# Which matmuls are cut into column halves, and where beta is transposed

## The chip, the cores and the metric

The kernel runs on one core of a Trainium2 chip. The metric is the device time of one execution in microseconds, and a kernel's figure is the median of its runs. Before the change the median of three runs is 275.47 us (275.43 to 276.7).

A core has a matrix engine (TensorE, PE in the profile; its weight loads are listed as PEld), a vector engine (VectorE, DVE), a scalar engine (ScalarE, ACT), GpSimd (POOL) and a sync engine (SyncE, SP) that here only issues transfers. Transfers run on 16 DMA engines that all queues share.

## What is computed

The reference is an attention without softmax, followed by a two-layer network with a gated activation:

```python
def phi(x, c, s):
    r = np.maximum(x, 0.0)
    return np.concatenate([r * c, r * s], axis=-1)
q_p = phi(q, cos_w, sin_w)
k_p = phi(k, cos_w, sin_w)
kv = np.einsum('bhsf,bhsd->bhfd', k_p, v)
z = np.sum(k_p, axis=2)
num = np.einsum('bhsf,bhfd->bhsd', q_p, kv)
den = np.einsum('bhsf,bhf->bhs', q_p, z)[..., None] + 1e-06
...
x = np.ascontiguousarray(attn_out.transpose(0, 2, 1, 3)).reshape(B * S, H * D)
h = x @ w_in
g = h * (1.0 / (1.0 + np.exp(-beta * h)))
out = g @ w_out
```

There are 8 batches of 8 heads, 576 positions and a head size of 64; the network has 4608 tokens, 512 inputs, 2048 hidden units and 512 outputs. Everything comes in and goes out as 32-bit floats; the matrix work is done in bf16.

## The kernel before

The 4608 tokens are worked off in nine chunks of 512 (`c` = 0 to 8). While the network works on one chunk, the attention for later tokens is prepared, so that matmuls of both kinds follow each other in one hand-written order on TensorE. The kernel switches the scheduler off (`manual_schedule`): each engine runs its instructions in the order in which the Python code records them. From chunk 1 on the order is a list of short tokens (`ORDERS`), read from left to right.

The matmuls that matter here:

- `kv_mm` (line 285) and `num_mm` (line 308) are the attention. They are small: 64 rows by 64 columns of weights, 130 or 65 columns of data, 36 or more in a row. Four of them run side by side in the matrix array, so they follow each other every 5 to 20 ns.
- `h_mm` (line 400) is the first layer of chunks 0 and 1. A hidden group of 128 units takes four matmuls (`mi` = 0 to 3) into one PSUM bank of 512 columns. The parameter `cols` cuts each of them but the first into that many column pieces; with `cols` = 2 a group is one matmul of 512 columns and six of 256. Lines 921 and 942 call it with 2 for the slots 4 to 15 of both chunks.
- `o_mm` (line 559) is the second layer of chunk 0, in parts of four hidden groups (`o_part`, slots 16 to 23). `cols` works in the same way, the first hidden group excepted. Line 923 asks for 2 in slots 16 to 22 and for 1 in slot 23.
- `o_fast` (line 581) is the second layer of chunk 1, and `o_pair` (line 631) that of the chunks 2 to 8. Both use a scheme that replaces eight block products by seven. A chunk has two row pairs (`pr` = 0 and 1, the tokens `x…`/`y…` in chunk 1 and `ox…`/`oy…` later). A product is eight matmuls of 256 columns that add up in half a PSUM bank; `prod` records them, and the products of a pair come in the order 1, 2, 6, 5, 7, 3, 4 or one like it.
- `h_pair` (line 524) does the first layer of chunks 2 to 8 in the same scheme, with products of two matmuls.

Each matmul is preceded by a load of its weights, an instruction of its own. Cutting a matmul into two pieces therefore adds two instructions to TensorE's stream.

The head of the kernel works as follows. TensorE runs small matmuls on zeros (`warm_pe`) until the table of tangents is ready. It then transposes that table (line 699) and, from a 16 by 128 tile, `beta` (line 702), runs 15 more warming matmuls, and turns the first two groups of queries (`q_turn_pe`, line 244) with one more warming matmul between them. VectorE copies the transposed `beta` out of PSUM (line 706), relus the second query group, multiplies the turned queries by the tangents (line 232), inverts `beta` (line 713) and goes on with values and keys (lines 218 and 201). The tile of `beta` arrives by a transfer that ScalarE issues (line 139). Its first users are the activations of the first layer (line 408) and the scaling of the second weight matrix (line 131).

Of the kernel before, what the change touches and what calls it, by code (L numbers as in the profile page):

```python
# [16 lines left out]
P = 128  # L17
NQ = 9
EPS = 1e-6


@with_exitstack
def kernel(
# [453 lines left out]
    def fast_ops(left, right, prod, finish):  # L477
# [36 lines left out]
            "4": lambda: prod(at("b", 0), left(6), right(6), False),  # L514
        }, bank, at

    def h_pair(c, i):

        jt0 = 2 * i
        xt, n = xt_tile(c), NB // 2  # L520

        def prod(dst, l, r, start):
            for g in range(2):
                nc.tensor.matmul(dst, lhsT=l[:, g], rhs=r[:, :, g * HP : (g + 1) * HP], start=start and g == 0,  # L524
                                 stop=g == 1, skip_group_check=True)

        def w(f, jp):
            f += jt0 % 4
            return win[jt0 // 4][:, 2 * jp : 2 * jp + 2, f * P : (f + 1) * P]

        def x(jp, k_):
            return xt[:, k_ * n : (k_ + 1) * n, jp]

        s1, s2, s3, s4 = (w_sum(jt0, k_) for k_ in range(4))
        t1, t2, t3, t4 = (wx["x"][:, 4 * (c % 2) + k_] for k_ in range(4))
        lefts = (w(0, 0), s1, s2, w(0, 1), s3, s4, w(1, 1))
        rights = (x(0, 0), t1, t2, x(1, 0), t3, x(1, 1), t4)
        ops, bank, at = fast_ops(lefts.__getitem__, rights.__getitem__, prod, lambda add: add(at("b", 1)))
        ops["A"] = lambda: h_silu(c, jt0, bank("a"))
        ops["B"] = lambda: h_silu(c, jt0 + 1, bank("b"))  # L540
        return ops
# [32 lines left out]
    def o_fast(c, pr, banks):  # L574

        b_ps, a_ps, e_ps = ps[:, banks[0], 0:HM], ps[:, banks[1], 0:HM], ps[:, banks[1], HM:DM]
        tok = slice(pr * P, (pr + 1) * P)

        def prod(dst, left, right, start, stop):
            for i in range(JT // 2):  # L580
                nc.tensor.matmul(dst, lhsT=left(i), rhs=right[:, i], start=start and i == 0,  # L581
                                 stop=stop and i == JT // 2 - 1, skip_group_check=True)

        def g_part(r, hf):
            def at(i):
                jt = 2 * i + r
                return gs[c, jt // 4][:, jt % 4, hf * (TCH // 2) + pr * P : hf * (TCH // 2) + (pr + 1) * P]
            return at

        def s_part(t):  # L590
            return lambda i: t[:, i, tok]

        o1 = osb_pool.tile([P, DM], FP32, name="o_sb", tag="o_sb")
        o2 = osb_pool.tile([P, DM], FP32, name="o_sb", tag="o_sb")
        p1 = part.tile([P, HM], FP32, name="p1", tag="p1")
        p5 = part.tile([P, HM], FP32, name="p5", tag="p5")
        u = part.tile([P, HM], FP32, name="u", tag="u")

        add = dict(op=ALU.add)
        return {  # L600
            "1": lambda: prod(b_ps, g_part(0, 0), B11, True, False),
            "5": lambda: prod(e_ps, s_part(S[1]), T1, False, False),
            "6": lambda: prod(b_ps, s_part(S[2]), T2, False, False),
            "2": lambda: prod(a_ps, g_part(1, 0), B21, True, True),
            "7": lambda: prod(b_ps, s_part(S[3]), T3, False, False),
            "3": lambda: prod(e_ps, s_part(S[4]), B22, False, True),
            "4": lambda: prod(b_ps, g_part(1, 1), T4, False, True),
            "c1": lambda: nc.scalar.copy(p1, b_ps),
            "c5": lambda: nc.scalar.copy(p5, e_ps),
            "cu": lambda: nc.scalar.copy(u, b_ps),  # L610
            "c4": lambda: nc.scalar.copy(o2[:, 0:HM], b_ps),
            "a2": lambda: nc.vector.tensor_tensor(o1[:, 0:HM], a_ps, p1, **add),
            "a3": lambda: nc.vector.tensor_tensor(o1[:, HM:DM], e_ps, u, **add),
            "a7": lambda: nc.vector.tensor_tensor(o2[:, HM:DM], b_ps, p5, **add),
            "o1": lambda: store(c, pr, o1),
            "o2": lambda: store(c, pr + 2, o2),
            "p1": lambda: store(c, pr, o1, eng=nc.sync),
            "p2": lambda: store(c, pr + 2, o2, eng=nc.sync),
        }


    def o_pair(c, pr):

        last = c == NTC - 1 and pr == 1
        tok = slice(pr * P, (pr + 1) * P)
        order = (0, 1, 2, 3, 4, 5, 7, 6) if c + 1 >= B else range(JT // 2)
        sb = {}

        def prod(dst, l, r, start):
            for i in order:  # L630
                nc.tensor.matmul(dst, lhsT=l(i), rhs=r[:, i], start=start and i == 0, stop=i == order[-1],  # L631
                                 skip_group_check=True)

        def g_part(r, hf):
            def at(i):
                jt = 2 * i + r
                return gs[c, jt // 4][:, jt % 4, hf * (TCH // 2) + pr * P : hf * (TCH // 2) + (pr + 1) * P]
            return at

        def s_part(t):  # L640
            return lambda i: t[:, i, tok]

        def sb_tile(key):
            sb[key] = osb_pool.tile([P, DM], FP32, name="o_sb", tag="o_sb")
            return sb[key]

        def stored(half):
            sb["done"] = sb.get("done", 0) + 1
            if last:
                store(c, pr + 2, sb["2"], half * HM, (half + 1) * HM)  # L650
            elif sb["done"] == 2:
                store(c, pr + 2, sb["2"])

        def finish(add):
            add(sb_tile("2")[:, HM:DM])
            stored(1)

        def piece(half, eng):
            if "1" not in sb:
                sb_tile("1")  # L660
            cols = slice(half * HM, (half + 1) * HM)
            (nc.scalar.copy if eng == "act" else nc.vector.tensor_copy)(sb["1"][:, cols], at("a", half))
            store(c, pr, sb["1"], half * HM, (half + 1) * HM)

        def take(key, eng):
            copy = nc.scalar.copy if eng == "act" else nc.vector.tensor_copy
            if key == "a":
                got = copy(sb_tile("1"), bank("a"))  # L668
                store(c, pr, sb["1"])
            else:  # L670
                got = copy(sb["2"][:, 0:HM], at("b", 0))
                stored(0)
            return got

        lefts = (g_part(0, 0), s_part(S[1]), s_part(S[2]), g_part(1, 0), s_part(S[3]), s_part(S[4]), g_part(1, 1))
        rights = (B11, T1, T2, B21, T3, B22, T4)
        ops, bank, at = fast_ops(lefts.__getitem__, rights.__getitem__, prod, finish)
        ops["A"], ops["B"] = (lambda: take("a", "act")), (lambda: take("b", "act"))
        ops.update({n: lambda h=i % 2, e=("act", "dve")[i // 2]: piece(h, e) for i, n in enumerate("PQUV")})
        ops["X"], ops["Y"] = (lambda: take("a", "dve")), (lambda: take("b", "dve"))  # L680
        return ops
# [2 lines left out]
        for i in range(count):  # L684
            nc.tensor.matmul(ps[:, bank, 0:w], lhsT=zeros[:, 0:P], rhs=zeros[:, 0:w], start=True, stop=True)  # L685

    def warm_long(count):
        for i in range(count):
            nc.tensor.matmul(ps[:, 1], lhsT=zeros.bitcast(FP32)[:, 0:P],
                             rhs=raw_tile(0, "q")[:, 0, 0:8].rearrange("q n d -> q (n d)"), start=True, stop=True)  # L690

    beta = const.tile([P, JT], FP32, name="beta")
    rbeta = const.tile([P, JT], FP32, name="rbeta")

    warm_pe(54, 48)

    for bank, n0, n1 in ((6, 0, 5), (7, 5, NQ)):
        for n in range(n0, n1):
            nc.tensor.matmul(ps[:, bank, (n - n0) * HP : (n - n0 + 1) * HP],
                             lhsT=tan9[0:HP, n : n + 1].to_broadcast([HP, P]), rhs=identf,  # L700
                             is_transpose=True, start=(n == n0), stop=(n == n1 - 1))
    nc.tensor.transpose(ps[:, 1, 0:JT], beta16, identf[0:JT, 0:JT])
    for bank, n0, n1 in ((6, 0, 5), (7, 5, NQ)):
        nc.scalar.copy(tanr[:, n0:n1, :].rearrange("q n p -> q (n p)"), ps[:, bank, 0 : (n1 - n0) * HP])
    q_relu(0, 0)
    nc.vector.tensor_copy(beta, ps[:, 1, 0:JT])
    nc.vector.tensor_copy(ps[:, 0, 0:NQ], cos9)
    nc.vector.tensor_copy(ps[:, 0, 16 : 16 + NQ], sin9)
    q_relu(0, 1)
    warm_pe(6, 128, bank=2)  # L710
    warm_pe(9, 48, bank=2)
    q_turn_pe(0, 0, 4)
    nc.vector.reciprocal(rbeta, beta)
    warm_pe(1)
    take = q_turn_pe(0, 1, 2, hold=True)
    warm_long(2)
    take("act", 0)
    take("dve", 1)
    v_scale(0, 1, 0, 0, 8, eng="pool")
# [193 lines left out]
    for slot in range(32):  # L913
        if slot < 4:
            if slot == 0:
                for jt in range(2):
                    h_mm(0, jt, (2, 3), slice(0, 4))
            h_mm(0, slot, (2, 3), slice(4 if slot < 2 else 0, 8))
            h_act(0, slot)
        elif slot < 16:  # L920
            h_group(0, slot, 2 if slot < 16 else 1)
        elif slot < 24:
            o_part(0, slot % 4, (slot - 16) // 4, 2 if slot < 23 else 1)
        else:
            for tt in range(4):
                o_mm(0, tt, (slot - 16,))
# [10 lines left out]
    def h_slot(slot):  # L937
# [1 line left out]
            h_mm(1, slot, (2, 3))  # L939
            h_act(1, slot)  # L940
        else:
            h_group(1, slot, 2 if slot < 16 else 1)

    def behind_turn():
        for jp in range(2):
# [197 lines left out]
```

## Time and profile before

| what | us |
|---|---|
| median of three runs | 275.47 |
| lowest and highest run | 275.43 and 276.7 |
| the profiled execution's own time | 276.29 |
| its span, first to last instruction | 274.5 |
| TensorE busy in the span | 264.1 |
| VectorE busy | 225.9 |
| ScalarE busy | 196.3 |
| GpSimd busy | 57.0 |

The profiled execution is one run; 1.8 us of its time lie outside the span. Its costliest groups of instructions on TensorE, from the page:

```profile
L524 PE MATMUL ps<-w_stage,ws 128*128 128x256 bf16 x324 | 52.4, 273 | 0.0
L524 PE MATMUL ps<-xt,win 128*128 128x256 bf16 x216 | 37.0, 273 | 0.0
L631 PE MATMUL ps<-wout,g_t 128*128 128x256 bf16 x224 | 28.9, 273 | 0.0
L400 PE MATMUL ps<-xt,win 128*128 128x256 bf16 (+1 forms) x220 | 32.4, 306 | 0.0
```

A row names the line, the engine, what is written and read, and the shape; `x324` is the count, `52.4, 273` the busy time in us and the mean duration of one in ns, and the last number the idle time of the engine just before them. The duration of one matmul runs from its first read to its last write; matmuls overlap, so that 324 of 273 ns fill 52.4 us and not 88. What counts for the time is the distance from one start to the next.

The page also lists what the DMA queues moved. Two of them carry instructions, not data: `q8` with 30 packets of 16 KB and `q14` with 12 of 8 KB.

### The profile page before, as it was taken

How to read it: one execution, taken by the hardware profiler on the slowest of the kernel's cores; microseconds unless marked ns; L12 is line 12 of the kernel's file. 1: busy time of each engine (PE TensorE's matmuls, PEld its weight loads, DVE VectorE, ACT ScalarE, POOL GpSimd, SP SyncE). 2: the span in 40 equal slices, each digit the busy share in tenths (PEclk: the TensorE clock that was granted, in tenths of full speed). 3: DMA queues.
4: the chain of work that ended last, by engine and by line, in shares of the span. 5: the costliest groups of instructions: out<-in, count | busy, mean ns of one | idle time of the engine just before them, and what ended most of it. 6: DMA issues, size and time to landing. Idle time of an engine off the chain costs nothing.

```text
span 274.5 us, 9255 instructions
## 1 busy us (share of the span) xinstructions
PE 264.1 (96%) x3834; PEld 219.5 (80%) x3837; DVE 225.9 (82%) x596; ACT 196.3 (72%) x406; POOL 57.0 (21%) x75
## 2 busy tenths in 40 slices
PE   7799999999899999999999999989999999999994
PEld 6557775577686888888888888878888888888883
DVE  4888799999879989779989996998589868758852
ACT  5588888697648968799489967976696179428910
POOL 1420000120025000850093009300840060000000
PEclk9999999999999999999999999999999999999999
DMA  7999999999997997899499559962600660015005
GB/s 247 371 396 384 390 388 289 291 232 351 307 185 219 359 278 78 249 401 161 105 270 370 97 61 242 292 77 57 180 4 2 61 180 5 2 28 127 1 2 153
DMA packets 51754, 54.15 MB, mean 197 GB/s; under 512 B 31920, under 2 KB 32448, under 8 KB 51712
## 3 DMA queue, kind: packets, MB, share of 16 engines
q1 hardware_dynamic: 49120, 47.26, 66.0%
q0 software_dynamic: 2208, 6.03, 7.1%
q8 instruction: 30, 0.49, 0.8%
q10 hardware_dynamic: 384, 0.27, 0.4%
q14 instruction: 12, 0.10, 0.1%
HBM read 36.71 MB, written 9.44 MB: 168 GB/s over the span
## 4 chain that ended last, share of the span: by engine, by line
PE 92%; DVE 3%; DMA 2%; issue 1%; ACTq 0%; ACT 0%; DVEq 0%
PE ps L631 32%; PE ps L524 31%; PE ps L400 11%; PE ps L559 5%; PE ps L581 5%; PE ps L308 4%; PE ps L285 3%; DMA beta<-in_moe_beta_dram 2%; DVE qs L232 1%; DVE vb L218 1%; PE ps L244 1%; PE ps L368 1%; DVE rk L201 1%; PE ps L685 0%; DVE xs L331 0%
## 5 line engine op out<-in xcount | busy, mean ns | idle before, releaser
L434 ACT ACTIVATE g_t<-ps,beta 128x512 bf16<-128x512 f32 x108 | 68.1, 704 | 2.2 <-PE ps L524 1.9
L524 PE MATMUL ps<-w_stage,ws 128*128 128x256 bf16 x324 | 52.4, 273 | 0.0
L550 POOL DMA_DIRECT2D out_dram<-o_sb x46 | 24.7, 543 | 130.0 <-ACT o_sb L668 87.7
L631 PEld LDWEIGHTS <-w_stage 128*128 128x128 bf16 x448 | 43.4, 98 | 5.2
L524 PEld LDWEIGHTS <-ws 128*128 128x128 bf16 x432 | 41.8, 98 | 6.1
L500 DVE TENSOR_TENSOR ps<-ps,p 128x256 f32<-128x256 f32 x82 | 33.9, 429 | 11.8 <-ACT p L497 4.0
L524 PE MATMUL ps<-xt,win 128*128 128x256 bf16 x216 | 37.0, 273 | 0.0
L631 PEld LDWEIGHTS <-g_t 128*128 128x128 bf16 x336 | 32.3, 98 | 4.3 <-ACT g_t L434 0.4
L524 PEld LDWEIGHTS <-win 128*128 128x128 bf16 x324 | 31.5, 98 | 4.1
L400 PE MATMUL ps<-xt,win 128*128 128x256 bf16 (+1 forms) x220 | 32.4, 306 | 0.0
L493 ACT COPY ps<-ps 128x256 f32<-128x256 f32 x68 | 24.8, 386 | 8.0 <-PE ps L524 3.8
L232 POOL TENSOR_TENSOR qs<-qt,tanr 128x1152 bf16<-128x1152 bf16 (+2 forms) x10 | 16.7, 1676 | 66.3 <-ACT xt L373 33.0
L631 PE MATMUL ps<-wout,g_t 128*128 128x256 bf16 x224 | 28.9, 273 | 0.0
L400 PEld LDWEIGHTS <-win 128*128 128x128 bf16 x220 | 21.3, 98 | 9.2
L420 DVE TENSOR_TENSOR w_stage<-g_t 128x512 bf16<-128x512 bf16 x64 | 26.2, 429 | 2.1 <-ACT g_t L434 1.7
L226 ACT ACTIVATE vb<-raw_v,sin 128x256 bf16<-128x256 f32 (+1 forms) x62 | 27.6, 511 | 0.0
L408 ACT ACTIVATE g_t<-ps,beta 128x512 bf16<-128x512 f32 x36 | 23.5, 693 | 4.5 <-PE ps L400 4.4
L631 PE MATMUL ps<-wout,w_stage 128*128 128x256 bf16 x224 | 26.6, 273 | 0.0
L631 PE MATMUL ps<-T,w_stage 128*128 128x256 bf16 x224 | 26.6, 273 | 0.0
L331 DVE TENSOR_TENSOR xs<-ps,rden 128x768 bf16<-128x768 f32 (+4 forms) x26 | 24.3, 942 | 0.9 <-DVE rden L324 0.2
L228 DVE TENSOR_SCALAR vb<-raw_v,cos 128x256 bf16<-128x256 f32 x63 | 22.4, 391 | 0.0
L668 ACT COPY o_sb<-ps 128x512 f32<-128x512 f32 x12 | 6.9, 588 | 20.8 <-PE ps L631 20.8
(116 smaller groups left out, 416.5 us busy)
## 6 DMA issues: line engine op xcount, KB each, us to landing
raw_v<-in_v_dram SPq DMA_DIRECT2D x7, 1152.0 KB, 8.8
raw_k<-in_k_dram SPq DMA_DIRECT2D x7, 1152.0 KB, 11.6
raw_q<-in_q_dram SPq DMA_DIRECT2D x7, 1152.0 KB, 9.2
out_dram<-o_sb POOLq DMA_DIRECT2D x46, 128.0 KB, 4.8
w_stage<-in_moe_w_in_dram SPq DMA_DIRECT2D x6, 512.0 KB, 8.3
out_dram<-o_sb SPq DMA_DIRECT2D x22, 128.0 KB, 3.1
w_stage<-in_moe_w_out_dram SPq DMA_DIRECT2D x2, 1024.0 KB, 9.5
w_stage<-in_moe_w_out_dram SPq DMA_DIRECT2D x4, 512.0 KB, 13.8
```

Of the source, the lines that this page charges most:

```text
L226: got = nc.scalar.activation(o, a, AF.Copy, scale=t[:, n : n + 1])
L228: got = nc.vector.tensor_scalar(o, a, scalar1=t[:, n : n + 1], scalar2=None, op0=ALU.mult)
L331: nc.vector.tensor_tensor(o.rearrange("q j n s d -> q j (n s) d"), nv[:, :, a:z, :, 0:D].rearrange("q j n s d -> q j (n s) d"), rden[:, :, ...
L400: nc.tensor.matmul(ps[:, h_bank(c, jt), i * 64 : (i + w) * 64], lhsT=win[jt // 4][:, mi, (jt % 4) * P : (jt % 4 + 1) * P], rhs=xt[:, i : i ...
L408: return nc.scalar.activation(gs[c, jt // 4][:, jt % 4], ps[:, h_bank(c, jt)], AF.Silu, scale=beta[:, jt : jt + 1])
L420: return nc.vector.tensor_tensor(o, l, r, op=op)
L434: return nc.scalar.activation(gs[c, jt // 4][:, jt % 4], bank, AF.Silu, scale=beta[:, jt : jt + 1])
L493: return nc.scalar.copy(at("a", 0), at("b", 0))
L500: nc.vector.tensor_tensor(dst, at("b", 0), st["p5"], op=ALU.add)
L524: nc.tensor.matmul(dst, lhsT=l[:, g], rhs=r[:, :, g * HP : (g + 1) * HP], start=start and g == 0, stop=g == 1, skip_group_check=True)
L550: (eng or own).dma_start(out=out_v[bb, n][:, m0:m1], in_=o_sb[hf * HP : (hf + 1) * HP, m0:m1])
L631: nc.tensor.matmul(dst, lhsT=l(i), rhs=r[:, i], start=start and i == 0, stop=i == order[-1], skip_group_check=True)
```

## The change

A table at the head names the places where matmuls are cut in two; all others stay whole.

```diff
+FINE = {("h", 0): (4, 5, 12),
+        ("h", 1): (4, 6, 8, 11, 13, 14, 15),
+        ("o", 0): (20, 21, 22, 23),
+        ("p", 1, 0): (5, 6, 7),
+        ("p", 1, 1): (5, 7),
+        ("p", 3, 0): (5, 6, 7),
+        ("p", 3, 1): (4, 5, 6, 7),
+        ("p", 5, 0): (5,),
+        ("p", 5, 1): (3,)}
...
+    made = {}
+
+    def product_width(c, pr, kind="p"):
+
+        made[kind, c, pr] = made.get((kind, c, pr), 0) + 1
+        return HM // 2 if made[kind, c, pr] in FINE.get((kind, c, pr), ()) else HM
...
         def prod(dst, left, right, start, stop):
+            w = product_width(c, pr)
             for i in range(JT // 2):
-                nc.tensor.matmul(dst, lhsT=left(i), rhs=right[:, i], start=start and i == 0,
-                                 stop=stop and i == JT // 2 - 1, skip_group_check=True)
+                for m0 in range(0, HM, w):
+                    nc.tensor.matmul(dst[:, m0 : m0 + w], lhsT=left(i), rhs=right[:, i, m0 : m0 + w],
+                                     start=start and i == 0 and m0 == 0, stop=stop and i == JT // 2 - 1,
+                                     skip_group_check=True)
...
-    warm_pe(54, 48)
+    warm_pe(63, 48)
...
-    nc.tensor.transpose(ps[:, 1, 0:JT], beta16, identf[0:JT, 0:JT])
...
     q_relu(0, 0)
-    nc.vector.tensor_copy(beta, ps[:, 1, 0:JT])
...
     q_turn_pe(0, 0, 4)
+    warm_pe(1, bank=7)
+    take = q_turn_pe(0, 1, 2, hold=True)
+    nc.tensor.transpose(ps[:, 1, 0:JT], beta16, identf[0:JT, 0:JT])
+    nc.vector.tensor_copy(beta, ps[:, 1, 0:JT])
     nc.vector.reciprocal(rbeta, beta)
-    warm_pe(1)
-    take = q_turn_pe(0, 1, 2, hold=True)
-    warm_long(2)
+    warm_long(2, bank=7)
...
-            h_group(0, slot, 2 if slot < 16 else 1)
+            h_group(0, slot, 2 if slot in FINE.get(("h", 0), ()) else 1)
...
-            o_part(0, slot % 4, (slot - 16) // 4, 2 if slot < 23 else 1)
+            o_part(0, slot % 4, (slot - 16) // 4, 2 if slot in FINE.get(("o", 0), ()) else 1)
...
-            h_group(1, slot, 2 if slot < 16 else 1)
+            h_group(1, slot, 2 if slot in FINE.get(("h", 1), ()) else 1)
```

`o_pair` and `h_pair` get the same loop as `o_fast`. The table counts the products of a pair in the order in which they are recorded: `("p", 3, 0): (5, 6, 7)` are the last three of the seven products of pair 0 in chunk 3. `h_pair` asks for the kind `"H"`, which the table doesn't have, so its products stay whole.

In the order of the program, in groups and products:

| place | cut before | cut after | instructions added |
|---|---|---|---|
| warming matmuls at the head | | 9 more | +18 |
| chunk 0, first layer, slots 6 to 11, 13 to 15 | 9 groups of 3 matmuls | whole | −54 |
| chunk 0, second layer, slots 16 to 19 | 4 parts of 3 matmuls | whole | −24 |
| chunk 0, second layer, slot 23 | whole | 4 matmuls | +8 |
| chunk 1, first layer, slots 5, 7, 9, 10, 12 | 5 groups of 3 matmuls | whole | −30 |
| chunk 1, second layer | whole | 5 products of 8 matmuls | +80 |
| chunk 3, second layer | whole | 7 products of 8 | +112 |
| chunk 5, second layer | whole | 2 products of 8 | +32 |

Together 50 matmuls of 512 columns that were two are one again, and 112 matmuls of 256 columns become 224 of 128. TensorE's stream gets 142 instructions longer; the order of the other engines' instructions changes only in the head, where VectorE's copy of `beta` moves from before the second relu to just before the inversion. No transfer is added, taken away or moved.

## What was predicted

> **What bounds the kernel now.** I read the page first, then the waits of TensorE, the timeline around its longest ones, the counts by stretch of time, and the chain through the head.
>
> ```profile
> span 274.5 us, 9255 instructions
> ...
> q8 instruction: 30, 0.49, 0.8%
> ...
> PE 92%; DVE 3%; DMA 2%; issue 1%; ACTq 0%; ACT 0%; DVEq 0%
> ```
>
> TensorE carries 92% of the chain that ended last. From 19.9 us on its matmuls start at an even distance, which I take from rows with many alike: 56 matmuls of 256 columns in 6.11 us of the chain, 109.2 ns each; and from the timeline the two rows below, (2.54 − 0.38) / 10 = 216 ns for 512 columns and (0.94 − 0.22) / 13 = 55.4 ns for 128 (0.38 and 0.22 are the lengths of the last one; read finely, 56).
>
> ```profile
> 40.05 2.54 PE L559 MATMUL ps<-wout,g_t 128*128 128x512 bf16 x11 [0.16 <-issue]
> 42.42 0.94 PE L244 MATMUL ps<-ident,qb 128*128 128x128 bf16 x14
> ```
>
> So two things can change the time: the number of columns streamed (which stays) and TensorE's waits. Its waits (total, times, longest):
>
> ```profile
> PE ps L308 <- issue: 2.4, 2, 1.3
> PE ps L685 <- DVE zero_b L157: 1.0, 1, 1.0
> PE ps L699 <- DVE tan L184: 0.7, 1, 0.7
> ...
> PE ps L702 <- DMA beta<-in_moe_beta_dram: 0.2, 1, 0.2
> ```
>
> The largest isn't for data: "issue" means that nothing recorded ended it. It sits in the middle of two runs of small matmuls:
>
> ```profile
> 72.92 0.20 PE L308 MATMUL ps<-kv,qs 64*64 64x65 bf16 x2
> ...
> 74.41 0.22 PE L308 MATMUL ps<-kv,qs 64*64 64x65 bf16 x2 [1.29 <-issue]
> ...
> 180.27 0.21 PE L308 MATMUL ps<-kv,w_stage 64*64 64x65 bf16 x4
> 181.58 0.22 PE L308 MATMUL ps<-kv,qt 64*64 64x65 bf16 x4 [1.10 <-issue]
> ```
>
> From start to start this costs 1.47 us (72.94 to 74.41) and 1.27 us (180.31 to 181.58), 2.74 together. Why there? TensorE's instructions between the two stops, matmuls and weight loads:
>
> ```profile
> 74.20:181.40 107.20, 106.07 (x1663) 91.16 (x1664) 94.81 (x246) 85.45 (x186) 33.12 (x34) 1.00 0.94 221
> ```
>
> 1663 + 1664 = 3327. TensorE's 7671 instructions against the 30 packets of queue q8 give 256 per packet, and 13 × 256 = 3328: both stops lie at the same place of a block of 256 instructions. The packets' times in the trace fit. The 8th went from 71.89 to 72.83 and TensorE went on 1.58 us later; the 21st from 179.18 to 180.37, and it went on 1.21 us later. Nothing else waits so close behind a packet: the 5th, 11th and 15th landed 1.37, 1.59 and 1.51 us before the first instruction of their block. I conclude that a packet is asked for about when TensorE enters the block before, that it queues with the data, and that its instructions can run some 1.2 to 1.6 us after it landed. Counting back 256 instructions from each stop, the block before began at 68.42 and 174.34; packet, transit and the rest took 5.99 and 7.24 us from there. Blocks of 256-column matmuls last 128 × 0.109 = 14 us and hide that; a block full of attention matmuls doesn't.
>
> [...]
>
> **The change part by part.**
>
> *Streaming.* 50 whole matmuls save 50 × (2 × 109.2 − 216) = 0.12 us. 112 cut ones cost 112 × (2 × 56 − 109.2) = 0.31 us. Net +0.19 us. Here 56 comes from runs of 14 with a weight load before each; if longer runs were held by the loads (98 ns each in the page's rows) it would be 224 × 98 − 112 × 109.2 = +9.7 us. I take +0.19: the runs of 14 also load 14 times.
>
> *The head.* The chain there:
>
> ```profile
> 5.48 0.28 PE ps L702
> 5.77 1.11 PE ps L685 x15
> 6.88 0.97 PE ps L244 x9
> 7.95 1.35 DVE qs L232 x2
> 9.30 0.23 DVE rbeta L713
> ```
>
> TensorE waits for beta's tile (landed 5.44). Moved behind the turns, this leaves the last tangent transpose (start 4.96) followed by the 15 matmuls at about 5.06 instead of 5.70: the first turn ends 0.64 us sooner. Its relu is done at 5.63 and doesn't hold it. VectorE is then the chain to 15 us; the copy of beta (0.17 busy) now stands in it before the inversion: −0.64 + 0.15 = −0.49 us. Its later inputs landed earlier than it needs them (values 7.88 and 10.9, keys 9.4). The nine more warming matmuls (9 × 40 ns = 0.36 us) lie in the wait of 0.7 us for the tangents: nothing, or +0.36 without that cover. Range −0.65 to +0.36.
>
> *The blocks.* By the table of the change the first stop's place is reached with 18 − 54 − 24 + 8 − 30 = 82 instructions fewer before it, the second's with 82 − 80 − 112 = −110, that is 110 more. Both block ends move against the work:
> - 8th packet: its block now ends 82 instructions later, after the 36 left of the attention run and 46 (23 matmuls) of 256 columns. The block before starts in the same fast run (0.3 us later in the work) and lasts 6.70 us without a stop; 5.99 are needed. Stop of 1.47 gone; worst 0.5 left.
> - 21st: its block before starts 110 instructions sooner, at 166.3 on the new clock, and lasts 11.5 us; 7.24 needed. Stop of 1.27 gone.
>
> The same shift brings other block ends into attention runs. I laid the old start times under the new order; the tight ones, with room, need by the same packet's own delay before, and need by the worst delay (7.24):
>
> | packet | new room | need, own | need, worst | taken |
> |---|---|---|---|---|
> | 2nd (used at 21.7) | 6.5 | 6.4 to 6.8 | 7.24 | 0.2 |
> | 4th (44.7, first sevens of batch 1) | 6.25 | 3.3 to 3.7 | 7.24 | 0.2 |
> | 7th (67.9) | 7.0 | 6.2 | 7.24 | 0 |
> | 8th (74.6) | 6.7 | 6.0 | 7.24 | 0 |
> | 18th (150.8) | 6.0 | 3.9 to 4.3 | 7.24 | 0 |
> | 22nd (183.9) | 6.1 | 3.8 to 4.2 | 7.24 | 0.3 |
> | 25th (205.8) | 5.9 | 3.0 to 3.4 | 7.24 | 0 |
>
> 11th and 15th keep their rooms (4.5 and 5.3 us), in which they made it. The 4th's block now starts inside a run, so that it is asked for later in the work than before, and the 22nd queues behind transposes that the 21st met before; hence a bit above nothing. Taken 0.7 us, at worst 0.7 + 1.0 + 0.2 + 0.5 + 1.2 + 1.1 + 1.3 = 6.0.
>
> *Behind the stops.* While TensorE stood, the others worked on: at 72.78 ScalarE had itself idled 1.31 us for TensorE, so it isn't late next. At 88.6 and 93.2 TensorE waits 0.1 us for VectorE; I leave that.
>
> *Sum.* −2.74 + 0.19 − 0.49 + 0.7 = −2.34 us. The profiled execution took 276.29 us (span 274.5 and 1.8 around it), so 273.95 for its like. It lies 0.82 above the median of 275.47; if the whole gain carries over, the median becomes 273.1, if the 0.82 is part of the stops, 273.95. I say 273.5.
>
> **Rivals.**
>
> *R1, the stop moves.* The 4th packet is asked for at 38.4, while the DMA engines are busy throughout (share about 1.0 until 42), and its block ends in the middle of 224 fast instructions. If it or the 22nd comes as late as packets did in the worst, with 1 to 1.1 us each, the gain is eaten to 275.47 − 2.34 + 1.6 = 274.7: no change. For: room of 6.25 and 6.1 against 7.24 seen. Against: most packets came within 4 us of the block's start.
>
> [...]
>
> *R3, the stops don't depend on the place* (they come from the transfers of that moment: raw keys land at 72.4 and 179.4). Then only head and streaming are left: 275.47 − 0.30 = 275.2.
>
> *R4, slower: many packets late.* A block of 128-column products lasts 128 × 0.056 = 7.2 us instead of 14, and an attention run in it still less, so that packets 18, 22 and 25 come due sooner than before. If all seven tight ones take the worst time, the stops are 6.0 us: 275.47 − 3.04 + 6.0 = 278.4; it decides from 3.04 us of new stops on. For: the 21st and 8th took 7.24 and 5.99. Against: the DMA engines are nearly idle from 199 to 212, and the seven would have to be late together.
>
> **How the numbers follow.** Forecast 0.55 (own range 272.4 to 274.6), R1 0.17, R2 0.06, R3 0.14, R4 0.08. Low end 275.47 − 2.74 − 0.65 + 0.19 = 272.3; high end 276.4 leaves out R2 and half of R4. About 0.5% (1.4 us) is what a measurement can tell from no change. Faster by more (under 274.1): most of the forecast and a little of R1, 0.55. Slower (over 276.85): R2 and part of R4, 0.12. Between: 0.33.
>
> **What would show it.** Right: no "issue" wait of TensorE above 0.5 us on line 308, q8 still 30 or 31 packets; the first turn of queries ends near 7.3 us; 128-column products start every 56 ns. Wrong: an "issue" wait of 1 us or more at another place 256 × n instructions on (R1), one at the same work (R3), or a distance above 66 ns in line 581 or 631 (R2).

## The result, and the profile after

The changed kernel takes 273.2 us (median of 6 runs, 272.46 to 273.68), against 276.73 for the kernel before on the same chips (6 runs, 275.43 to 277.3): a ratio of 0.9882, 95% interval 0.9852 to 0.9912. The profiled execution took 273.17 us, in the middle of its kernel's runs; that of the kernel before took 276.29. Ratios, here and below, leave out runs more than 1.5% above the fastest of the same kernel; medians and ranges hold all runs.

The page of the changed kernel, its head and the shares of the chain that ended last:

```profile
span 271.4 us, 9399 instructions
...
q8 instruction: 30, 0.49, 0.7%
...
PE 91%; DMA 5%; DVE 1%; ACT 1%; ACTq 0%; issue 0%; DVEq 0%; SPq 0%
```

The span is 3.1 us shorter with 142 instructions more (144 by the records, of which a few are missing); the packets of instructions are still 30; the chain's share of "issue" went from 1% to 0%. TensorE's waits (what it waited for: total us, times, longest), now complete:

```profile
PE ps L709 <- DVE zero_b L166: 1.0, 1, 1.0
PE ps L317 <- ACT kv L304: 0.5, 1, 0.5
PE ps L723 <- DVE tan L193: 0.4, 1, 0.4
PE ps L578 <- DVE wout L140: 0.2, 1, 0.2
```

No wait for "issue" is left. One wait is new: line 578 (the second layer of chunk 0, 559 before) for VectorE's scaled weights. The timeline of TensorE at the places of the two old stops (start, length, engine, line, operands, count, and in brackets the idle time before):

```profile
72.46 0.21 PE L317 MATMUL ps<-kv,qs 64*64 64x65 bf16 x4
72.50 0.21 PE L317 MATMUL ps<-kv,qt 64*64 64x65 bf16 x4
72.53 0.21 PE L317 MATMUL ps<-kv,qs 64*64 64x65 bf16 x4
72.67 1.05 PE L602 MATMUL ps<-T,w_stage 128*128 128x256 bf16 x8
...
74.53 0.83 PE L602 MATMUL ps<-wout,w_stage 128*128 128x128 bf16 x12
```
```profile
177.98 0.20 PE L317 MATMUL ps<-kv,w_stage 64*64 64x65 bf16 x4
178.01 0.20 PE L317 MATMUL ps<-kv,qt 64*64 64x65 bf16 x4
178.05 0.20 PE L317 MATMUL ps<-kv,w_stage 64*64 64x65 bf16 x4
```

Both attention runs go through without a bracket. The last row of the first fence is a cut product: (0.83 − 0.22) / 11 = 55 ns from start to start. The chain through the head (start, length, what):

```profile
4.07 1.19 PE ps L723 x9
5.27 1.11 PE ps L709 x15
6.38 0.96 PE ps L253 x9
7.34 0.43 PE ps L709
7.77 0.96 PE ps L253 x9
8.73 0.21 PE ps L737
8.94 2.73 PE ps L713 x4
11.67 0.70 PE ps L294 x36
...
12.40 0.39 ACT kv L304
```

The tangents' transposes (723) are followed at once by the 15 warming matmuls and the first query turns, which end at 7.34 us; beta's transpose (737) stands behind the second turns. VectorE's piece of 1.35 us for the first product and that for the inversion are no longer in the chain of this execution.

I laid the start times of the matmuls of both traces, one execution of each kernel, beside each other in the order of the program. The step of each stretch, in us:

| stretch | predicted | measured |
|---|---|---|
| head, up to the first matmul of the first layer (17.72, now 16.91) | −0.49 | −0.81 |
| whole groups and cut products | +0.19 | +0.1 |
| TensorE late at 42.7 (for scaled weights) and 45 (for turned queries) | 0 | +0.59 |
| small stop at 50.3, 5th packet | 0 | −0.23 |
| stop at 72.9 | −1.47 | −1.46 |
| stop at 180.3 | −1.27 | −1.30 |
| new stops (2nd, 4th, 22nd packet) | +0.7 | 0 |
| all, rest included | −2.34 | −3.07 |

### The profile page after: what moved, and what is told of

The parts are those of the page before. It is cut to its first block, busy times and chain, and to the rows that moved or that the text cites. A ratio compares the mean times of both kernels' runs of the same rounds, so it can differ in the third digit from the quotient of the medians.

```text
span 271.4 us, 9399 instructions
## 1 busy us (share of the span) xinstructions
PE 265.2 (98%) x3908; PEld 216.6 (80%) x3908; DVE 225.2 (83%) x596; ACT 196.3 (72%) x406; POOL 57.0 (21%) x75
## 4 chain that ended last, share of the span: by engine, by line
PE 91%; DMA 5%; DVE 1%; ACT 1%; ACTq 0%; issue 0%; DVEq 0%; SPq 0%
PE ps L655 32%; PE ps L542 31%; PE ps L409 10%; DMA w_stage<-in_moe_w_out_dram 5%; PE ps L602 5%; PE ps L317 4%; PE ps L294 3%; PE ps L578 2%; PE ps L713 1%; PE ps L253 1%; PE ps L377 1%; PE ps L709 1%; ACT L173 0%; PE ps L723 0%; DVE xs L340 0%
## 5 line engine op out<-in xcount | busy, mean ns | idle before, releaser
L655 PEld LDWEIGHTS <-w_stage 128*128 128x128 bf16 x504 | 44.3, 98 | 4.6
L542 PEld LDWEIGHTS <-win 128*128 128x128 bf16 x324 | 31.4, 98 | 4.0
L409 PE MATMUL ps<-xt,win 128*128 128x512 bf16 (+1 forms) x178 | 32.3, 338 | 0.0
L409 PEld LDWEIGHTS <-win 128*128 128x128 bf16 x178 | 17.1, 98 | 12.6
L655 PE MATMUL ps<-wout,w_stage 128*128 128x256 bf16 (+1 forms) x264 | 26.7, 256 | 0.0
L655 PE MATMUL ps<-T,w_stage 128*128 128x256 bf16 (+1 forms) x240 | 26.6, 266 | 0.0
L237 DVE TENSOR_SCALAR vb<-raw_v,cos 128x256 bf16<-128x256 f32 x63 | 21.7, 378 | 0.0
```

Source lines behind the costliest of these rows:

```text
L237: got = nc.vector.tensor_scalar(o, a, scalar1=t[:, n : n + 1], scalar2=None, op0=ALU.mult)
L409: nc.tensor.matmul(ps[:, h_bank(c, jt), i * 64 : (i + w) * 64], lhsT=win[jt // 4][:, mi, (jt % 4) * P : (jt % 4 + 1) * P], rhs=xt[:, i : i ...
L542: nc.tensor.matmul(dst[:, m0 : m0 + w], lhsT=l[:, g], rhs=r[:, m0 // HP : (m0 + w) // HP, g * HP : (g + 1) * HP], start=start and g == 0 a ...
L655: nc.tensor.matmul(dst[:, m0 : m0 + w], lhsT=l(i), rhs=r[:, i, m0 : m0 + w], start=start and i == 0 and m0 == 0, stop=i == order[-1], skip ...
```

## The experiments

The theory, from the first trace of before: every 256 TensorE instructions (7671 over 30 packets) need a packet of queue q8, which is asked for at about the time when the block before begins (there it goes out 0.9 us before to 4.8 us after that), queues with the data and can be used 1.2 us or more after it landed (1.21 us at the stop at 180); a stop appears where a block runs through its instructions sooner than that. Line numbers differ by a few between kernels: 308, 309 and 317 are the same matmuls of the attention, 581 and 594 the same products as 602, 631 and 647 those of 655.

In what follows the times of packets are worked out from the traces: the start of a block is that of the matmul 256 × n instructions on from the first stop; "out" and "landed" are the packet's record on q8; "used" is the first matmul of the next block.

That stops stand at block ends is exact: in the ten traces that can be read, every `issue` wait of TensorE above 0.16 us falls at weight load 734, 1118, 1502, 2014 or 2782 of the stream (counted from 0). These lie 384, 384, 512 and 768 loads apart, all multiples of 128 loads, that is of 256 instructions.

### The head alone

Before's cuts, with beta's transpose behind the query turns (and still 54 warming matmuls):

```diff
-    nc.tensor.transpose(ps[:, 1, 0:JT], beta16, identf[0:JT, 0:JT])
-    nc.vector.tensor_copy(beta, ps[:, 1, 0:JT])
...
+    warm_pe(1, bank=7)
     take = q_turn_pe(0, 1, 2, hold=True)
+    nc.tensor.transpose(ps[:, 1, 0:JT], beta16, identf[0:JT, 0:JT])
+    nc.vector.tensor_copy(beta, ps[:, 1, 0:JT])
     nc.vector.reciprocal(rbeta, beta)
```

> Only the head is changed (beta's transpose behind the turns, 54 warming matmuls as before); the cuts are those of before, so the stream has as many instructions as before and every block of 256 ends at the same work. Theory (a stop comes where a block ends inside attention matmuls): TensorE reaches the first layer 0.7 to 0.8 us sooner, both 'issue' stops stay, near 72.2 and 179.5 us, 1.0 to 1.7 us each; 0.7 us under before. Rival 'it is all the head': 3 us under before and no stops. Rival 'stops come from the transfers of the moment, not the place': as the theory here.

Median 276.06 us, ratio to before 0.9982 [0.9949, 1.0015]; 0.7 us less than before was expected. The first layer begins at 16.92 us, as in the changed kernel (16.91), so the nine more warming matmuls there make no difference. TensorE's waits in its profile (span 273.3):

```profile
PE ps L309 <- issue: 1.0, 1, 1.0
...
PE ps L369 <- issue: 0.6, 1, 0.6
```

The stop at 73 is still there (1.24 us from start to start). The one at 180 isn't: the 21st packet was out 2.2 us after its block's start, not 4.8. A stop of 0.83 us stands at 49.6 in its place, where the 5th packet now comes too late: TensorE reached that block end sooner. The earlier the first layer begins, the longer this stop: 0.29 us where it begins at 17.72 (before), 0.44 at 17.47 (before, second profile), 0.79 at 17.01 (before without its first stores), 0.83 at 16.92 here. So the gain of the head is partly given back 30 us later, and what is left of it can't be told from nothing.

### The plan alone

The table of the change with the head of the kernel before.

> Only the plan of cuts, with the head of before; the stream is 18 instructions shorter than that of after. Theory: the block that the 8th packet brings is first needed 7.1 us after the block before it began, the 22nd 6.1 us: no stop of 1 us or more; 18th and 25th with 5.0 us may lose up to 0.5 each. 2.5 us under before (2.74 less 0.19), to 1.5 with the small ones. Rival 'not the place': both stops stay and the time is 0.2 us over before. Rival 'it is all the head': as before.

Median 274.49 us, ratio 0.9942 [0.9905, 0.9979]. The profiled execution took 278.67 us, 4.2 more than the median; one other of the ten took 278.25. (The stop below and the slower clock behind it, see the last section, come to about 4.8 us.) Nothing stops at 73 or 180; the timeline at 100:

```profile
100.49 0.22 PE L309 MATMUL ps<-kv,qt 64*64 64x65 bf16 x3
103.74 0.21 PE L309 MATMUL ps<-kv,qt 64*64 64x65 bf16 x1 [3.02 <-issue]
```

This is the end of the 11th block. Its packet went out 4.90 us after the block's start (96.19 to 101.09), landed at 102.23 and was used 1.51 us later. In the kernels before and after it went out after 1.92 us. The plan takes the old stops away; a new one can appear at the 11th.

### Without the cut products

The table without its `"p"` entries, so that the block ends from chunk 1 on lie elsewhere.

```diff
-        ("p", 1, 0): (5, 6, 7),
-        ("p", 1, 1): (5, 7),
-        ("p", 3, 0): (5, 6, 7),
-        ("p", 3, 1): (4, 5, 6, 7),
-        ("p", 5, 0): (5,),
-        ("p", 5, 1): (3,)}
+        }
```

> The change without its cut products of the second layers (chunks 1, 3 and 5 whole; the head and the cuts of chunks 0 and 1's groups as in after). Up to 77 us it is the same program, from there on 80, then 192, then 224 instructions shorter. Theory: no stop at 72; the 21st packet's block is needed 4.5 us after the one before began, at about 181.4, where before it took 7.2: a stop of 1 to 2.7 us inside the attention matmuls there; 11th (3.7 us of room) and 14th (4.4) may lose up to 0.8. In all 1.3 to 3 us over after, 0 to 2 under before. Rival 'not the place': no difference from after but the 0.3 us of the cuts. Rival 'cut products by themselves help': a stop at both places of before.

The profiled execution of this first run took 949.64 us. In its timeline

```profile
300.35 3.68 PE L534 MATMUL ps<-w_stage,ws 128*128 128x256 bf16 x8
```

matmuls of 256 columns start every (3.68 − 1.0) / 7, about 0.4 us, instead of 0.109. Nothing about packets can be read from it. The other runs give a ratio of 1.0041 [0.9978, 1.0103]. So the kernel was run again:

> The kernel of e3 once more, whose profiled execution ran with TensorE at a quarter of its speed throughout and can't be read. Theory as there: none at 72; a stop of 1 to 2.7 us inside the attention matmuls at about 181 (21st packet, 4.5 us of room), up to 0.8 at 99 (11th, 3.7 of room) and at 124 (14th, 4.4); 1 to 3 us over after. Rival 'not the place': as after less 0.3.

Median 277.17 us, ratio 1.0018 [0.9974, 1.0062], and the profiled execution is a plain one (span 273.6). Its timeline at 100:

```profile
99.96 0.20 PE L309 MATMUL ps<-kv,qt 64*64 64x65 bf16 x2
102.25 0.22 PE L309 MATMUL ps<-kv,qt 64*64 64x65 bf16 x2 [2.09 <-issue]
```

The expectation is missed in place: nothing at 181, where the block end has returned to the attention run (the packet was out 0.08 us before its block began, and was used 3.6 us after it landed), but 2.28 us at the 11th block's end, whose packet went out after 3.09 us. So a block that TensorE runs through quickly isn't enough for a stop: its packet has to be late too. What the cut products buy is their instructions: without these the gain of head and first layer isn't to be seen in the time.

### The same matmuls, cut elsewhere

Two kernels have exactly the matmuls of the changed kernel; only other products of the same pairs are cut, which moves the block ends between.

```diff
-        ("p", 1, 0): (5, 6, 7),
-        ("p", 1, 1): (5, 7),
+        ("p", 1, 0): (1, 2, 3),
+        ("p", 1, 1): (1, 2),
```

> The same matmuls as after, of the same shapes and as many: only which products of chunk 1 are cut differs, the 1st, 2nd and 3rd of pair 0 and the 1st and 2nd of pair 1 (66 to 72 us) where after cuts the last ones (77 to 82 us). Theory: at 72 us the 80 added instructions lie ahead, so the 8th packet's block ends inside the attention matmuls again, needed 4.3 us after the block before began, where 6.0 were taken before: a stop of 1.3 to 1.8 us near 72.2, and the time that much over after. The later places are as in after: no second stop. Rival 'not the place' and rival 'it is the head or the cutting': as after, within 0.3 us.

Median 274.58 us, ratio 0.9941 [0.9914, 0.9968]. The 8th block's end is back in the attention run, and so is the stop, 1.59 us from start to start:

```profile
72.36 0.19 PE L309 MATMUL ps<-kv,qs 64*64 64x65 bf16 x3
73.95 0.21 PE L309 MATMUL ps<-kv,qs 64*64 64x65 bf16 x1 [1.40 <-issue]
```

```diff
-        ("p", 3, 0): (5, 6, 7),
-        ("p", 3, 1): (4, 5, 6, 7),
+        ("p", 3, 0): (1, 2, 3),
+        ("p", 3, 1): (1, 2, 3, 4),
```

> The same matmuls as after, as many and of the same shapes; only which products of chunk 3 are cut differs (the first three of pair 0 and the first four of pair 1 in place of the last). Theory: 72 us as in after, no stop; the 15th packet's block is now needed 2.7 us after the one before began, at 126.4, and in after it took 2.0 to its start, 1.0 to land and at least 1.2 more: a stop of 1.5 to 2.5 us at 126, and the time that much over after. Behind it all as in after. Rival 'not the place': as after within 0.3.

Median 277.49 us, ratio 1.0046 [1.0011, 1.0081]. Nothing at 73; the stop is at the 15th block's end, in a cut product behind attention runs:

```profile
126.02 0.61 PE L647 MATMUL ps<-wout,g_t 128*128 128x128 bf16 x8
129.90 0.51 PE L647 MATMUL ps<-wout,g_t 128*128 128x128 bf16 x6 [3.27 <-issue]
```

The place is the one worked out beforehand; the size, 3.49 us from the last start of the block before, is above the 1.5 to 2.5 expected. The packet went out 3.84 us after its block's start (2.0 in the changed kernel) and was used 1.32 us after it landed. Same matmuls, same head: 1.4 us more in one case, 4.3 in the other (medians against 273.2). Which products are cut, and so where the block ends fall, decides which packet comes too late.

### Fewer transfers before the stop

The kernel before without the stores of chunk 0's rows (four tokens taken out of chunk 1's order), which are in flight when the 8th packet is asked for (in before eight transfers of 128 KB, issued from 60.4 to 64.2 us and landed 6.8 to 10.5 us later).

> The kernel of before without the stores of chunk 0's result (four row blocks, eight transfers of 128 KB, issued between 60 and 64 us and landed by 74); the rows stay unwritten. TensorE's stream is the same. Theory (the packet queues behind data): about 1 MB less in front of the 8th packet, some 2.6 us at 400 GB/s, so it goes out 1 to 2.6 us earlier than 71.9 and the stop at 73 shrinks from 1.5 to 0 to 0.5 us; the second stop, where there is one, stays. Rival 'a fixed delay from the block's start': packet at 3.5 us after the start as before, stop of 1.3 to 1.5.

Median 275.14 us, ratio 0.9979 [0.9951, 1.0008]. The same work, the same block end, and in the timeline:

```profile
72.99 0.19 PE L308 MATMUL ps<-kv,qs 64*64 64x65 bf16 x2
73.51 0.22 PE L308 MATMUL ps<-kv,qs 64*64 64x65 bf16 x2 [0.33 <-issue]
```

The stop is 0.52 us instead of 1.48. The block began at 68.35 as before (68.42), but the packet was out at 69.85 instead of 71.89. It then took 2.06 us to land instead of 0.93, so that it landed 0.92 us sooner, about what the stop lost. So the packet's way depends on the data in front of it; a fixed delay of the fetch would have left the stop as it was. This is one execution, but all the readable traces point the same way. For 47 packets the DMA engines were less than a tenth busy with other transfers around their block's start (0.5 us before it to 1 us after it): these went out 0.2 us before the start in the median and at most 1.7 us after it. For 171 packets they were over nine tenths busy: median 2.6 us after the start, longest 5.0.

The ratio can't be told from 1, and the same execution stops at three other block ends: 0.79 us at the 5th packet, 0.46 us at the 15th and 0.87 us at the 21st. Of its list of waits:

```profile
PE ps L308 <- issue: 1.0, 2, 0.7
...
PE ps L368 <- issue: 0.6, 1, 0.6
```

### Both kernels once more

> The kernel of before once more, for a second profile: which stops are there each time. Theory: a stop at 73 every time (room 4.5 us, 6.0 needed), of 1 to 2 us; the one at 180 (room 6.0) depends on when the transposes pass and may be missing. Rival 'the stops are an accident of one execution': none at either place, or at other places that are no multiple of 256 instructions away.

One run, 274.92 us, span 273.1. The stop at 73 is there (1.50 us; `issue` in the timeline for 1.30), the one at 180 isn't: the 21st packet was out 2.50 us after its block's start, 2.3 sooner than in the first profile. The second stop is not in every execution.

> The changed kernel once more, for a second profiled execution of it. By the theory (block ends away from dense work, the packet's way out varies by the data in front of it) the 8th block's end near 68.2 and the 21st's near 178.0 show no issue wait over 0.3 us; the 11th packet, whose start-to-out delay was 1.6 us in the changed kernel's first profile and 3.1 and 4.9 us in the two neighbouring plans that stopped there, may show one: no stop if its delay is under 2 us, a stop of 1.5 to 3.5 us near 98 to 101 if it is over 3 us. By the rival (the changed plan has no place where a packet can be late) no issue wait over 0.3 us anywhere, whatever the delay. Span 271 to 272 without a stop, 273 to 275 with one.

273.38 and 273.80 us, span 271.6, no wait for "issue" in TensorE's list. The 11th packet went out 1.73 us after its block's start, so the two theories can't be told apart here. (In the first profile it was 1.92 us, not the 1.6 that the expectation names.)

The packets that matter, in us; "out" counts from the block's start, "under way" from out to landed, "used" from the landing:

| kernel | packet | block starts | out after | under way | used after landing | stop |
|---|---|---|---|---|---|---|
| before | 8th | 68.42 | 3.47 | 0.93 | 1.58 | 1.48 |
| before | 21st | 174.34 | 4.84 | 1.19 | 1.21 | 1.28 |
| before again | 5th | 44.86 | 2.85 | 1.10 | 1.46 | 0.44 |
| before again | 8th | 68.37 | 3.50 | 0.91 | 1.59 | 1.50 |
| before again | 21st | 174.31 | 2.50 | 1.65 | 1.82 | none |
| after | 7th | 61.05 | 4.67 | 0.88 | 1.61 | 0.13 |
| after | 8th | 68.21 | 3.28 | 0.95 | 2.42 | none |
| after | 11th | 94.49 | 1.92 | 1.10 | 1.51 | 0.11 |
| after | 21st | 166.50 | 4.27 | 0.96 | 6.29 | none |
| after | 22nd | 178.02 | 1.38 | 0.88 | 3.82 | none |
| head alone | 5th | 44.57 | 3.21 | 1.05 | 1.61 | 0.83 |
| head alone | 8th | 68.52 | 3.44 | 0.98 | 1.32 | 1.24 |
| plan alone | 11th | 96.19 | 4.90 | 1.14 | 1.51 | 3.24 |
| without cut products | 11th | 96.24 | 3.09 | 0.95 | 1.96 | 2.28 |
| cuts of chunk 1 moved | 8th | 67.99 | 3.73 | 1.02 | 1.21 | 1.59 |
| cuts of chunk 3 moved | 15th | 123.64 | 3.84 | 1.10 | 1.32 | 3.49 |
| before, without first stores | 5th | 44.43 | 3.07 | 1.51 | 1.25 | 0.79 |
| before, without first stores | 8th | 68.35 | 1.50 | 2.06 | 1.60 | 0.52 |
| before, without first stores | 15th | 125.22 | 2.41 | 1.91 | 1.36 | 0.46 |
| before, without first stores | 21st | 173.76 | 2.31 | 3.12 | 1.39 | 0.87 |

Here a stop is the gap from start to start at the block's end; 0.1 is the ordinary spacing there.

## Why the prediction was right, and where it wasn't

**The blocks.** Right in mechanism, place and size: −1.46 and −1.30 us against −1.47 and −1.27. The room of 6.70 and 11.5 us worked out for the 8th and 21st packets is 6.66 and 11.52 in the trace. That the place does it is shown by the two kernels with the same matmuls cut elsewhere; that the data in front of a packet makes it late, by the profile without the first stores and by the packets of all traces sorted by how busy the DMA engines were. The −1.30 us is the difference of the first profiles alone: the second profile of before has no stop there.

Packets went out between 1.0 us before the first matmul of the block before and 4.8 us after it in the first profiles of the two kernels, between 1.5 us before and 5.0 us after in all ten traces, never a block earlier; the stops in the table are 0.44 to 3.49 us long.

**New stops.** The term of +0.7 was too high: the 2nd, 4th and 22nd packets were used 2.01, 2.25 and 3.82 us after they landed. The 2nd went out 3.4 us after its block's start (4.2 in before). The 4th went out 3.4 us after it too, where it had taken 1.0 in before: that it would be asked for later in the work was right. Neither took the worst delay, and it was the weight given to that which put the term up. The 4th had some help: its room was 6.8 us instead of 6.25, because TensorE was late inside its block. But the seven tight packets listed don't name the right ones: the 7th, taken at 0, is used 1.61 us after landing, at the limit, and the 11th and 15th, which "keep their rooms", are where neighbouring plans stopped. That the own delay of a packet carries over to another plan is the weak step: the 11th's went from 1.9 to 3.1 and 4.9 us.

**The head.** Right in direction, and the first turns end at 7.34 us, as predicted (near 7.3). The size is less sure than −0.81 against −0.49 looks, because it compares single executions. With the old head the first layer begins at 17.72 us in the first profile of before, at 17.47 in the second and at 17.01 in that without the first stores; in the two profiles of the changed kernel it begins at 16.91 and 16.86. Between the second profiles the gain is 0.61 us.

The step that failed is "VectorE is then the chain to 15 us". In the first profile TensorE has every piece of the chain to 12.37, and the copy of beta isn't in it. In the second profile, and in that of the head alone, the copy and the inversion are in the chain, as predicted, but VectorE leaves it near 10 us; ScalarE's values and keys follow, and TensorE. From the chain of the second profile:

```profile
8.93 0.19 DVE beta L738
9.11 0.02 issue
9.14 0.25 DVE rbeta L739
9.39 0.56 DVE qs L241
...
10.92 0.63 ACT rk L209
11.54 0.04 issue
11.59 0.73 PE ps L294 x36
```

The nine more warming matmuls lie in the wait for the tangents, as said: it fell from 0.7 to 0.4 us.

**What was not foreseen.** TensorE, earlier by the head, now waits at 42.7 us for VectorE's scaled weights, and is late at 45 for turned queries: +0.59 us together. The prediction looked at what is late behind the old stops, not at what is late behind a faster head. The changed kernel's chain comes to that wait over a transfer of the second weight matrix, which is the DMA's 5% in its page:

```profile
28.25 13.91 DMA w_stage<-in_moe_w_out_dram
...
42.19 0.50 DVE wout L140
...
42.73 1.89 PE ps L578 x8
```

This transfer lands at 42.16 us here. It lands at 41.96 and 42.24 in the two profiles of before and at 42.10 with the head alone, so it doesn't move with the head. The chain of the head alone runs through it as well, though TensorE's idle time there is too short for the list of waits: the earlier head is enough to bring TensorE up against this transfer.

**Streaming.** +0.19 predicted, about +0.1 measured for whole groups (−0.06 to −0.1) and cut products (+0.2) together. In the 219 adjacent pairs of 128-column matmuls that the trace holds on lines 602 and 655, the distance has a median of 56 and a mean of 55.8 ns.

**The rivals.** R2 (loads hold the cut products; 0.06 in the forecast) is out by these 56 ns: from 66 ns on, 224 × 10 ns would have used up the predicted gain of 2.34 us, and no run shows cut products held by their loads. R3 (stops independent of the place) is out by the two kernels with moved cuts, though the transfers of the moment do decide how late a packet is. R1 and R4 didn't happen in the changed kernel. A stop that moves is real all the same: the plan alone and the kernel without cut products had one at the 11th packet, the kernel with chunk 3's cuts moved at the 15th.

**The median.** 273.5 was set between 273.1 (the whole gain carries over) and 273.95 (the 0.82 us by which before's profile lay above its median is part of the stops). Both are part of the truth. The second stop of before comes and goes, as its second profile shows: the gain against that execution is 1.7 us (274.92 − 273.2), against the first 3.1. That 273.5 came so near 273.2 is in part luck. It counts from the median of three runs, 275.47; the six runs beside the changed kernel have 276.73, so that the measured gain is 3.53 us, where the forecast's medians had 1.97. The terms that were off, −0.32 in the head, +0.59 behind it, −0.23 at the 5th packet, −0.7 for the new stops, leave −0.66 in the sum; the nearness of the medians hides this.

**What stays open.** Why the 11th packet's way out takes 1.6 us in one run (cuts of chunk 1 moved) and 4.9 in another (plan alone): all its cases begin between 94.4 and 96.3 us, and no experiment held the transfers of that moment fixed. So it isn't shown that the changed kernel never stops there, only that two profiles of it don't and that its eight runs lie between 272.46 and 273.80 us.

## What to carry to other kernels

Where an engine runs small instructions densely, look for waits that nothing recorded ends, divide its instruction count by the number of instruction packets (here 7671 by 30), and see whether the waits lie at multiples of that block; then the number of instructions ahead of a dense run is a tuning knob, and cuts that cost almost nothing elsewhere (here +0.2 us for 112) can turn it. Judge a plan by the room of every block against the worst delay of any packet, not against the delay that the same packet had before, because moving one block end moves all behind it (the 11th packet's went from 1.9 to 3.1 and 4.9 us). A head made faster is worth only what the next late producer, transfer or packet lets through (here −0.81 us, then +0.59). And where a wait comes and goes between executions, take a second profile of both kernels before a step is called mis-sized.

## What was not expected of the hardware

After the two longest stops, of 3.0 and 3.3 us idle, the granted clock was lower: 0.50 over 3.1 us behind the first, 0.59 and then 0.72 over 2.1 and 3.0 us behind the second. Behind the stops of 1.3 us (before), 1.4 us (chunk 1's cuts moved) and 2.1 us idle it was 1.00; over the span it is 0.994 in these two traces and 0.997 to 1.000 in the others. Counts by stretch (the last three numbers are granted clock, DMA share and GB/s), first the plan alone, then chunk 3's cuts moved (stop of 3.3 us), then the kernel without cut products (stop of 2.1 us):

```profile
102.40:104.40 2.00, 0.66 (x46) 0.59 (x47) 0.00 (x0) 2.00 (x6) 0.00 (x0) 0.95 1.01 168
104.40:107.50 3.10, 3.10 (x16) 2.20 (x15) 1.27 (x4) 1.75 (x4) 0.00 (x0) 0.50 0.15 29
```
```profile
129.90:132.00 2.10, 2.10 (x23) 2.10 (x24) 0.00 (x0) 0.00 (x0) 0.00 (x0) 0.59 1.08 78
132.00:135.00 3.00, 3.00 (x34) 2.50 (x33) 1.08 (x4) 2.15 (x5) 0.00 (x0) 0.72 0.07 7
```
```profile
102.30:104.30 2.00, 2.00 (x31) 1.78 (x32) 0.69 (x3) 2.00 (x5) 0.00 (x0) 1.00 0.03 8
```

In the plan alone 16 matmuls of 256 columns then start every 213 ns instead of 109, from 104.2 to 107.6 us: behind this stop of 3.0 us the lower clock cost about 1.7 us more (16 × 104 ns). How long an idle time brings the lower clock is not shown, only that 3.0 and 3.3 us were followed by it and 2.1 us was not.

The execution of 949.64 us is the other surprise: its matmuls are at about a quarter of the usual pace throughout, while its records show a granted clock of 1.00. One execution of one kernel did this; its cause is open.
